# Moving the additions of the output halves: from the head of the next tick to the tail of the tick of the copies

## The chip, the cores and the metric

The kernel runs on one core of one Trainium2 chip. The metric is the device time of one execution in microseconds (us): 1191.49 us is the median of three runs of the kernel before, which lie between 1190.52 and 1192.2 us. The traces come from a profiled execution of its own. The engines are named as in the profile: PE (TensorE matrix products), PEld (its weight loads), DVE (VectorE), ACT (ScalarE), POOL (GpSimd) and SP (SyncE, which only issues DMAs).

## The reference

The kernel computes windowed attention followed by a gated feed-forward layer, all in float32. The attention has 8 batches, 8 heads, 576 positions and a head size of 64. Half of the heads see a plain window of 32 positions, the other half a dilated one (every fourth position, 128 back).

```python
scores = scale * np.matmul(q, k.transpose(0, 1, 3, 2))
scores = np.where(masks[None, :, :, :], scores, -1000000000.0)
scores = scores - np.max(scores, axis=-1, keepdims=True)
attn = np.exp(scores)
attn = attn / (np.sum(attn, axis=-1, keepdims=True) + 1e-09)
attn_out = np.matmul(attn, v)
# 4608 tokens of 512 features: heads side by side
rms = np.sqrt(np.mean(x * x, axis=-1, keepdims=True) + 1e-06)
xn = x / rms * rms_g
g = xn @ w_gate                       # 512 -> 1536
val = xn @ w_val                      # 512 -> 1536
out = (g / (1 + np.exp(-g)) * val) @ w_out   # 1536 -> 512
```

## The kernel before, in words

**Units and ticks.** The 4608 tokens are cut into 16 units of 288 tokens (half a batch each). The feed-forward layer of unit u and the attention of unit u+1 are interleaved: while TensorE multiplies with the weights of unit u, the attention of the next unit is threaded in between. The order of everything is written out by hand in the Python program. Time there is counted in ticks: a tick is one block of feed-forward products on TensorE, either `gate` (a product with a piece of w_gate, PSUM bank "g"), `val` (the same with w_val, bank "v") or `proj` (the product with a piece of w_out, four accumulators). A unit has 12 pieces and so 36 ticks.

**Order within a tick.** `later(dt, rank, fn)` puts work off to the tick dt ahead. At the start of a tick, `flush()` issues what was put off to it, in the order of the ranks; then come the tick's products on TensorE and behind them the attention's products (`attend` and `products`). As each engine works through its own instructions in the order of issue, the ranks set the order of DVE, ACT and POOL.

**Attention.** It runs in bursts, 14 per unit: one burst is a pair of heads and 72 or 96 queries. From unit 3 on a burst starts every second tick; in unit 2 every one or two ticks. For a burst whose scores are made in tick q:

- tick q: scores on TensorE (line 428), into PSUM tile `s`
- tick q+1, rank 0.7: `scores_max` on DVE (lines 307 and 312)
- tick q+2, rank 2: `scores_exp` on ACT (line 322)
- tick q+4, rank -1: `scores_norm`, a small addition and a reciprocal on DVE (lines 329 and 330) and the scaling on POOL (line 332)
- tick q+5: the transposes on TensorE (line 402), into the unused part of the bank "g" or "v"; tick q+6, rank 0.2: `untranspose`, a rounded copy on ACT (line 385) and the remainder on DVE (line 387)
- tick q+8: the product with the values on TensorE (lines 416 and 417), into PSUM tile `o`, of which there is one
- tick q+9, rank 0.5: `take` on ACT (line 357), below

**Halves.** Operands of the products are split into a part in the rounded format fp32r ("hi") and a remainder ("lo"). The product of the probabilities with the values leaves two halves side by side in `o`: that of the hi part and that of the lo part. `take` copies the second half on ACT to the SBUF tile `xraw` (two copies of 64 partitions, one per head), and DVE adds the first half to it (two additions, line 350). After that `o` is free for the next burst's product.

**Other work of DVE that the prediction speaks of.** `prod` (line 603, rank 0) multiplies gate and value, `silu` (line 590, rank 0.8) finishes the gate's activation, `q_lo` (line 290, rank 0.9) makes the remainder of the queries, and `split_weight` (line 187, rank 6) makes the remainder of a weight piece; the last stands on POOL or DVE, and only until all the weights are split, in the time of units 0 to 2. The transposes go to the bank that `silu` or `prod` reads, and are held until these have read it. The first two units compute in plain float32 and have no halves to add.

Of the kernel before, what the change touches and what calls it, by code (L numbers as in the profile page):

```python
# [14 lines left out]
ALU = mybir.AluOpType  # L15
PSUM = bass.MemoryType.PSUM

B, H, S, D = 8, 8, 576, 64
# [6 lines left out]
DIL = 4  # L25
QB = 96
NC = DM // P
NJ = FF // P
NNAT = 2
# [15 lines left out]
def geometry(u, c):  # L45


    half = u % 2
    if c < NC // 2:
        if half:  # L50
            return [(QB * i, QB * i, 0, P) for i in range(U // QB)], QB, U + W
        return [(QB * i, max(QB * i - W, 0), 0 if i else W, P if i else QB)
                for i in range(U // QB)], QB, U
    nq = U // DIL
    keys = nq + (W if half else 0)
    return [(nq * r, keys * r, 0 if half else W, keys) for r in range(DIL)], nq, keys * DIL
# [3 lines left out]
def attn_moe(ctx: ExitStack, tc: tile.TileContext, qk_in, v_in, w_gate, w_val, w_out, rms_g, outT):  # L60
# [4 lines left out]
    V, A, G, PE = nc.vector, nc.scalar, nc.gpsimd, nc.tensor  # L65
# [32 lines left out]
    def later(dt, rank, fn):  # L98
        put_off.setdefault(now[0] + dt, []).append((rank, fn))
# [123 lines left out]
    def load_v(b):  # L223

        if b is not None and b[0] >= NNAT:
            u, c, i = b
            vt = sb.tile([P, 2, D], F32, tag="vt", name=f"vt_{u}_{c}_{i}", bufs=3)
            nc.sync.dma_start(out=vt.rearrange("p a d -> p (a d)"), in_=v_in[u, c][:, i * 2 * D:(i + 1) * 2 * D])
            vs[b] = vt

    def further(b, n):

        k = everything.index(b) + n
        return everything[k] if k < len(everything) else None
# [6 lines left out]
    def split_v(b, dt):  # L241
        k = everything.index(b) % 2

        def hi():
            if k not in vparts:
                vparts[k] = [late[0].tile([P, 2, D], F32R, name=f"v{p}_{k}", bufs=1) for p in ("hi", "lo")]
            A.copy(out=vparts[k][0], in_=vs[b])  # L247

        def lo():
            vh, vl = vparts[k]  # L250
            G.tensor_tensor(out=vl, in0=vs.pop(b), in1=vh, op=ALU.subtract)  # L251
            load_v(further(b, 3))

        later(dt, 3.3, hi)
        later(dt, 5.1, lo)

    def after(u, h, n):

        k = u * H + h + n
        return divmod(k, H) if k < NU * H else None  # L260
# [37 lines left out]
    st, xraw, xsq = {}, {}, {}  # L298
# [36 lines left out]
    def take(u, c, i, o):  # L335

        blocks, nq, _ = geometry(u, c)
        if (u, c) not in xraw:
            xraw[u, c] = sb.tile([P, U], F32, tag="xraw", name=f"xraw_{u}_{c}", bufs=NC)
        x = xraw[u, c]  # L340
        if c < NC // 2:
            to = x[:, QB * i:QB * i + nq]
        else:
            to = x.rearrange("p (j r) -> p r j", r=DIL)[:, i, :]
        copy = V.tensor_copy if i % 2 and u != 1 else A.copy

        def add():
            for a in range(2):
                rows = slice(a * D, (a + 1) * D)
                V.tensor_tensor(out=to[rows], in0=o[rows, a * nq:(a + 1) * nq], in1=to[rows], op=ALU.add)  # L350

        if u < NNAT:
            for a in range(2):
                copy(out=to[a * D:(a + 1) * D], in_=o[a * D:(a + 1) * D, a * nq:(a + 1) * nq])
        else:
            for a in range(2):
                A.copy(out=to[a * D:(a + 1) * D], in_=o[a * D:(a + 1) * D, (2 + a) * nq:(3 + a) * nq])  # L357
            later(1, -0.5, lambda: add())
        if i == len(blocks) - 1:
            later(1, 2.5, lambda: square(u, c))  # L360

    def square(u, c):
        first = c == 0
        sq = sb.tile([P, U], F32, tag="xsq" if first else "tmp", name=f"sq_{u}_{c}", bufs=1 if first else 2)
        x = xraw[u, c]
        A.activation(out=sq, in_=x, func=AF.Square)
        if u == 0:
            G.tensor_scalar(out=x, in0=x, scalar1=gs[:, c:c + 1], scalar2=1.0, op0=ALU.mult, op1=ALU.mult)
        if first:
            xsq[u] = sq  # L370
        else:
            later(1, 0.4, lambda: (V if c == NC - 1 else G).tensor_tensor(out=xsq[u], in0=xsq[u], in1=sq, op=ALU.add))
# [6 lines left out]
    def untranspose(b, t_ps):  # L379
        blocks, nq, _ = geometry(*b[:2])  # L380
        n = blocks[b[2]][3]
        t_in = t_ps[:n].rearrange("k (a q) -> k a q", a=2)[:, :, :nq]
        exact = b[0] < NNAT
        st[b] = pt = sb.tile([P, 2, 2, QB], F32 if exact else F32R, tag="pt", name=f"pt_{b[0]}_{b[1]}_{b[2]}", bufs=2)
        A.copy(out=pt[:n, 0, :, :nq], in_=t_in)
        if not exact:
            V.tensor_tensor(out=pt[:n, 1, :, :nq], in0=t_in, in1=pt[:n, 0, :, :nq], op=ALU.subtract)  # L387

    def products(q, t, o, t_ps, s_tag="s", o_tag="o"):


        if q:
            s_ps = ps.tile([P, 512], F32, tag=s_tag, name=f"s_{q[0]}_{q[1]}_{q[2]}")
        if o:
            o_ps = ps.tile([P, 512], F32, tag=o_tag, name=f"o_{o[0]}_{o[1]}_{o[2]}")
            pt = st.pop(o)
        if t:
            p, _ = st.pop(t)
        def transposed(a):
            blocks, nq, _ = geometry(*t[:2])  # L400
            n = blocks[t[2]][3]
            PE.transpose(t_ps[:n, a * QB:a * QB + nq], p[:nq, a, :n], ident[:nq, :nq])  # L402

        def output(a):
            blocks, nq, _ = geometry(*o[:2])
            n = blocks[o[2]][3]
            if a:
                return
            out = o_ps[:, :2 * nq].rearrange("d (a q) -> d a q", a=2)
            if o[0] < NNAT:  # L410
                PE.matmul(out, vs.pop(o)[:n].rearrange("k a d -> k (a d)"), pt[:n, 0, :, :nq], start=True, stop=True)
                return
            vh, vl = (part[:n].rearrange("k a d -> k (a d)") for part in vparts[everything.index(o) % 2])

            both = o_ps[:, :4 * nq].rearrange("d (t a q) -> d t a q", t=2, a=2)
            PE.matmul(both, vh, pt[:n, :, :, :nq], start=True, stop=False)  # L416
            PE.matmul(out, vl, pt[:n, 0, :, :nq], start=False, stop=True)

        def scored(a):
            blocks, nq, _ = geometry(*q[:2])  # L420
            qc, kc, _, n = blocks[q[2]]
            sv = s_ps[:QB].rearrange("q (a t k) -> q a t k", a=2, t=2)
            if q[0] < NNAT:
                qr, kr = heads[q[0], 2 * q[1] + a]
                PE.matmul(sv[:nq, a, 0, :n], qr[:, qc:qc + nq], kr[:, kc:kc + n], start=True, stop=True)
                return
            qs, ks = heads[q[0], 2 * q[1] + a]
            PE.matmul(sv[:nq, a, :, :n], qs[:, qc:qc + nq], ks[:, :, kc:kc + n], start=True, stop=True)  # L428

        parts = [(b, fn, a) for b, fn in ((t, transposed), (o, output), (q, scored)) for a in range(2)]  # L430
        for b, fn, a in parts:
            if b:
                fn(a)
        if t:
            later(1, 0.2, lambda: untranspose(t, t_ps))
        if o:
            later(1, 0.5, lambda: take(*o, o_ps))
            if o[0] < NNAT:
                later(1, 9, lambda: load_v(further(o, 3)))
            far = further(o, 2)  # L440
            if far and far[0] >= NNAT:
                split_v(far, 8 if o[0] < NNAT else 1)
        if q:
            later(1, 0.7, lambda: scores_max(*q, s_ps))
            later(2, 2, lambda: scores_exp(*q))
            later(3 if q[0] < NNAT else 4, -1, lambda: scores_norm(*q))
            u, c, i = q
            nxt = after(u, 2 * c, 2)
            nb = len(geometry(u, c)[0])
            if u < NNAT:  # L450
                if u == NNAT - 1 and c == NC - 1 and i == nb - 1:
                    for a in range(2):
                        later(1, 9, lambda a=a: load(NNAT, a))
                        later(5 + a, 9, lambda a=a: split(NNAT, a, (1, 2, 2, 3), G, V))
            elif nxt and i == 0:
                split(*nxt, (1, 2, 2, 3), G, V)
                split(nxt[0], nxt[1] + 1, (2, 3, 3, 4), G, V)
# [224 lines left out]
    for n in range(ends):  # L682
# [8 lines left out]
        if n == ends - 1:  # L691
            _, v_free = gate(0, 0), val(0, 0)
# [101 lines left out]
```

## Time and profile before

| | |
|---|---|
| median of three runs | 1191.49 us (1190.52 to 1192.2) |
| the profiled execution's own time | 1190.96 us |
| its span, first to last instruction | 1189.2 us |
| busy: PE, DVE, ACT, POOL | 1131.2, 823.8, 720.1, 632.5 us |
| additions of the halves (line 350, DVE) | 392 instructions, 104.2 us busy |
| copies of the halves (line 357, ACT) | 392 instructions, 101.3 us busy |

In a row of the time order ("timeline"), the columns are the start in us, the duration in us, the engine, the line of the kernel, the operation, what it writes and reads, its shape, and how many instructions were merged in the row. Brackets at the end hold the engine's idle time before it, in us, and what it waited for. In a list of waits, the three numbers are the total in us, how often, and the longest.

### The profile page before, as it was taken

The page shows a single profiled execution, that of the slowest core. Times are in us where ns is not written, and L with a number is a line of the kernel's source. Part 1 is how long each engine was busy: PE and PEld are TensorE (multiplying, and loading weights), DVE is VectorE, ACT ScalarE, POOL GpSimd, SP SyncE. Part 2 cuts the span into 40 slices and gives each one's busy share as a digit, 9 for nine tenths or more (in the row PEclk, how much of TensorE's full clock was granted, in tenths as well). Part 3 has the DMA queues.
Part 4 walks back from the last instruction along what each step waited for, and adds up shares of the span by engine and source line. Part 5 has one row for each costly group of instructions (what it writes and reads, how often), then busy time and mean ns, then how long its engine had stood idle before and what let it go on. Part 6 is the DMA issues. An engine that isn't in the chain of part 4 may idle for free.

```text
span 1189.2 us, 25908 instructions
## 1 busy us (share of the span) xinstructions
PE 1131.2 (95%) x8296; PEld 1088.2 (92%) x8296; DVE 823.8 (69%) x2939; ACT 720.1 (61%) x2624; POOL 632.5 (53%) x1094
## 2 busy tenths in 40 slices
PE   4788888999999999999999999999999999999998
PEld 3566677999999999999999999999999999999998
DVE  4789786685858767586867767586776858687421
ACT  4667466675666657565765757566675756566321
POOL 2667466564556555464655646465554646455211
PEclk7699899999999999999999999999999999999999
DMA  5655322121312213121221212131121213120000
GB/s 151 196 181 200 93 73 58 34 85 34 92 40 79 58 38 91 37 80 39 69 60 50 88 33 75 40 89 49 48 83 34 81 37 93 40 76 17 1 21 21
DMA packets 62713, 82.19 MB, mean 69 GB/s; under 512 B 7442, under 2 KB 43282, under 8 KB 62578
## 3 DMA queue, kind: packets, MB, share of 16 engines
q1 hardware_dynamic: 61242, 79.60, 22.2%
q8 instruction: 66, 1.08, 0.4%
q10 hardware_dynamic: 1336, 0.94, 0.3%
q14 instruction: 69, 0.57, 0.2%
HBM read 71.08 MB, written 9.44 MB: 68 GB/s over the span
## 4 chain that ended last, share of the span: by engine, by line
PE 71%; DVE 18%; ACT 3%; DMA 3%; issue 2%; POOL 1%; SPq 0%; POOLq 0%; DVEq 0%; ACTq 0%
PE acc L551 7%; PE acc L552 7%; PE acc L553 7%; PE v L551 7%; PE g L551 7%; PE v L552 6%; PE v L553 6%; PE g L553 6%; PE g L552 6%; DVE qs L290 3%; PE o L416 3%; PE s L428 2%; DVE t L312 2%; DVE xraw L522 2%; PE g L402 2%
## 5 line engine op out<-in xcount | busy, mean ns | idle before, releaser
L615 POOL TENSOR_TENSOR hlo<-th,hhi 128x288 fp32r<-128x288 f32 x180 | 145.6, 809 | 230.0 <-ACT hhi L614 226.0
L332 POOL TENSOR_SCALAR t<-t,sm 96x128 f32<-96x128 f32 (+3 forms) x448 | 181.1, 416 | 85.3 <-DVE sm L330 58.6
L551 PE MATMUL v<-xhi,hi_v 128*128 128x288 f32 x720 | 220.5, 306 | 4.0 <-DVE pt L387 3.8
L551 PE MATMUL acc<-hhi,hi_o 128*128 128x288 f32 x720 | 221.0, 307 | 0.0
L551 PE MATMUL g<-xhi,hi_g 128*128 128x288 f32 x720 | 219.8, 305 | 0.3 <-DVE pt L387 0.2
L552 PE MATMUL acc<-hlo,hi_o 128*128 128x288 f32 x720 | 212.8, 296 | 0.2 <-POOL hlo L615 0.2
L552 PE MATMUL v<-xlo,hi_v 128*128 128x288 f32 x720 | 212.7, 295 | 0.0
L552 PE MATMUL g<-xlo,hi_g 128*128 128x288 f32 x720 | 212.7, 295 | 0.0
L553 PE MATMUL g<-xhi,lo_g 128*128 128x288 f32 x720 | 212.6, 295 | 0.0
L553 PE MATMUL acc<-hhi,lo_o 128*128 128x288 f32 x720 | 212.5, 295 | 0.0
L553 PE MATMUL v<-xhi,lo_v 128*128 128x288 f32 x720 | 212.3, 295 | 0.0
L614 ACT CAST hhi<-th 128x288 fp32r<-128x288 f32 x180 | 77.9, 433 | 169.6 <-DVE th L603 163.3
L322 ACT ACTIVATE t<-t,sm 96x128 f32<-96x128 f32 (+3 forms) x448 | 166.7, 375 | 16.4 <-DMA v<-in_v_dram 12.9
L251 POOL TENSOR_TENSOR vlo<-vt,vhi 128x128 fp32r<-128x128 f32 x196 | 94.1, 480 | 128.2 <-ACT vhi L247 104.1
L585 ACT ACTIVATE th<-g 128x288 f32<-128x288 f32 x180 | 73.9, 411 | 121.9 <-PE g L553 92.3
L551 PEld LDWEIGHTS v<-xhi,hi_v 128*128 128x128 f32 x720 | 135.2, 188 | 7.2 <-DVE pt L387 7.2
L350 DVE TENSOR_TENSOR xraw<-o,xraw 64x96 f32<-64x96 f32 (+1 forms) x392 | 104.2, 266 | 47.9 <-ACT xraw L357 45.0
L552 PEld LDWEIGHTS acc<-hlo,hi_o 128*128 128x128 f32 x720 | 135.8, 189 | 0.5 <-POOL hlo L615 0.5
L551 PEld LDWEIGHTS g<-xhi,hi_g 128*128 128x128 f32 x720 | 135.2, 188 | 0.6 <-DVE pt L387 0.3
L552 PEld LDWEIGHTS v<-xlo,hi_v 128*128 128x128 f32 x720 | 135.7, 188 | 0.0
L552 PEld LDWEIGHTS g<-xlo,hi_g 128*128 128x128 f32 x720 | 135.6, 188 | 0.0
L553 PEld LDWEIGHTS acc<-hhi,lo_o 128*128 128x128 f32 x720 | 135.4, 188 | 0.0
(120 smaller groups left out, 2668.1 us busy)
## 6 DMA issues: line engine op xcount, KB each, us to landing
qk<-in_qk_dram SPq DMA_DIRECT2D x56, 288.0 KB, 2.8
vt<-in_v_dram SPq DMA_DIRECT2D x196, 64.0 KB, 1.9
qk<-in_qk_dram SPq DMA_DIRECT2D x28, 352.0 KB
out_dram<-ot SPq DMA_DIRECT2D x64, 144.0 KB, 2.0
qk<-in_qk_dram SPq DMA_DIRECT2D x28, 304.0 KB, 2.8
raw_g<-in_w_gate_dram SPq DMA_DIRECT2D x12, 512.0 KB, 3.1
raw_v<-in_w_val_dram SPq DMA_DIRECT2D x12, 512.0 KB, 4.2
raw_o<-in_w_out_dram SPq DMA_DIRECT2D x12, 512.0 KB
```

The source lines that it names most:

```text
L251: G.tensor_tensor(out=vl, in0=vs.pop(b), in1=vh, op=ALU.subtract)
L290: eq.tensor_tensor(out=qs[D:], in0=qr[D:], in1=qs[D:], op=ALU.subtract)
L322: A.activation(out=t[:nq, a, :n], in_=t[:nq, a, :n], func=AF.Exp, scale=-1.0, bias=sm[:nq, a:a + 1], accum_out=sm[:nq, 2 + a:3 + a])
L332: G.tensor_scalar(out=t[:nq, a, :n], in0=t[:nq, a, :n], scalar1=sm[:nq, 2 + a:3 + a], scalar2=1.0, op0=ALU.mult, op1=ALU.mult)
L350: V.tensor_tensor(out=to[rows], in0=o[rows, a * nq:(a + 1) * nq], in1=to[rows], op=ALU.add)
L416: PE.matmul(both, vh, pt[:n, :, :, :nq], start=True, stop=False)
L551: PE.matmul(out, wh[:, cc, :], xh, start=start, stop=False)
L552: PE.matmul(out, wh[:, cc, :], xl, start=False, stop=False)
L553: PE.matmul(out, wl[:, cc, :], xh, start=False, stop=stop)
L585: A.activation(out=t, in_=g, func=AF.Tanh, scale=0.5)
L614: A.copy(out=hi, in_=t)
L615: G.tensor_tensor(out=lo, in0=t, in1=hi, op=ALU.subtract)
```

## The change

The two additions of a burst are no longer put off from `take` to the next tick at rank -0.5. They are put off, together with `take`, to the same tick as the copies, at rank 4. At the old place they stood behind `scores_norm` (rank -1) and ahead of everything else of tick q+10. At the new one they stand in tick q+9 behind `silu` and `q_lo`, ahead of the weight split (rank 6) of that tick, and ahead of `scores_norm` of tick q+10. What is added, and by which instructions, stays as it is, and for units 0 and 1 nothing differs.

```diff
@@ take
-
-        def add():
-            for a in range(2):
-                rows = slice(a * D, (a + 1) * D)
-                V.tensor_tensor(out=to[rows], in0=o[rows, a * nq:(a + 1) * nq], in1=to[rows], op=ALU.add)
-
         if u < NNAT:
             for a in range(2):
                 copy(out=to[a * D:(a + 1) * D], in_=o[a * D:(a + 1) * D, a * nq:(a + 1) * nq])
         else:
             for a in range(2):
                 A.copy(out=to[a * D:(a + 1) * D], in_=o[a * D:(a + 1) * D, (2 + a) * nq:(3 + a) * nq])
-            later(1, -0.5, lambda: add())
         if i == len(blocks) - 1:
             later(1, 2.5, lambda: square(u, c))
+
+    def add(u, c, i, o):
+        _, nq, _ = geometry(u, c)
+        x = xraw[u, c]
+        to = x[:, QB * i:QB * i + nq] if c < NC // 2 else x.rearrange("p (j r) -> p r j", r=DIL)[:, i, :]
+        for a in range(2):
+            rows = slice(a * D, (a + 1) * D)
+            V.tensor_tensor(out=to[rows], in0=o[rows, a * nq:(a + 1) * nq], in1=to[rows], op=ALU.add)
@@ products
         if o:
             later(1, 0.5, lambda: take(*o, o_ps))
+            if o[0] >= NNAT:
+                later(1, 4, lambda: add(*o, o_ps))
```

## The prediction

> **What bounds the kernel now.** I read the page first, then the busy times by stretch, then the waits of PE, then the time order around every wait of PE. The page says which engine is nearest to full:
>
> ```profile
> span 1189.2 us, 25908 instructions
> PE 1131.2 (95%) x8296; PEld 1088.2 (92%) x8296; DVE 823.8 (69%) x2939; ACT 720.1 (61%) x2624; POOL 632.5 (53%) x1094
> ```
>
> PE is busy 95% of the span, so a shorter time can come only out of PE's idle time. The busy times by stretch (window, its length, then busy time and instruction count of PE, PEld, DVE, ACT, POOL, the granted clock, the DMA share and GB/s) show where that is:
>
> ```profile
> 160.00:230.00 70.00, 61.29 (x454) 58.06 (x453) 47.69 (x168) 47.26 (x168) 43.13 (x71) 1.00 0.19 54
> 230.00:1110.00 880.00, 872.09 (x6721) 860.19 (x6721) 633.09 (x2352) 564.16 (x2119) 484.23 (x885) 1.00 0.20 59
> ```
>
> The additions are these (durations in ns: shortest, median, longest; first and last start):
>
> ```profile
> L350 DVE TENSOR_TENSOR xraw<-o,xraw x392: 226/261/298, 163.4 to 1110.6; 64x72 f32<-64x72 f32 x112, 64x96 f32<-64x96 f32 x84
> ```
>
> In the first stretch, where unit 2's attention runs together with the last weight splits, PE idles 70.00 - 61.29 = 8.71 us; in the 880 us behind it, 7.91 us. So 16.6 us is all that any change of this kind could win. The waits say how much of it hangs on the additions (rows of PE, then of DVE):
>
> ```profile
> PE o L416 <- DVE xraw L350: 4.5, 6, 1.4
> ...
> DVE xraw L350 <- ACT xraw L357: 45.0, 45, 1.8
> ```
>
> Six times the next burst's product with the values waits until the additions have read the one `o` tile: 4.5 us. The last row is the other side: at its old place the addition holds DVE 45 times, 45.0 us, for the copies of ACT. These are the single waits of PE that I go through below:
>
> ```profile
> 175.70 0.27 PE L402 MATMUL v<-ident,t 96*128 96x96 f32 x1 [0.64 <-DVE th L603]
> ...
> 183.68 0.41 PE L416 MATMUL o<-pt,vhi 128*128 128x384 f32 x1 [0.53 <-DVE xraw L350]
> ...
> 201.14 0.37 PE L416 MATMUL o<-pt,vhi 72*128 72x288 f32 x1 [0.30 <-DVE xraw L350]
> ...
> 205.41 0.37 PE L416 MATMUL o<-pt,vhi 72*128 72x288 f32 x1 [0.42 <-DVE xraw L350]
> ...
> 206.01 0.40 PE L551 MATMUL g<-xhi,hi_g 128*128 128x288 f32 x1 [0.17 <-DVE pt L387]
> ...
> 216.61 0.37 PE L416 MATMUL o<-pt,vhi 72*128 72x288 f32 x1 [1.40 <-DVE xraw L350]
> ...
> 526.72 0.41 PE L416 MATMUL o<-pt,vhi 128*128 128x384 f32 x1 [0.97 <-DVE xraw L350]
> ...
> 801.45 0.41 PE L416 MATMUL o<-pt,vhi 128*128 128x384 f32 x1 [0.83 <-DVE xraw L350]
> ```
>
> **The change, part by part.** No instruction is added or removed; 392 additions stay, and they issue no DMA and pass no work of SP, POOL or ACT. On DVE's queue they pass at most two things: a weight remainder (rank 6 of the tick of the copies) and the normalisation (rank -1 of the next tick). Where neither stands between the old and the new place, the order of DVE is word for word the same.
>
> *Past the weight remainders.* DVE's order around three of them:
>
> ```profile
> 172.34 0.43 DVE L590 SCALAR_TENSOR_TENSOR th<-th,g 128x288 f32<-128x288 f32 x1
> 173.53 1.10 DVE L187 TENSOR_TENSOR lo_g<-f_g,hi_g 128x512 fp32r<-128x512 f32 x1 [0.76 <-ACT hi_g L186]
> 174.55 0.51 DVE L350 TENSOR_TENSOR xraw<-o,xraw 64x96 f32<-64x96 f32 x2
> 175.10 0.46 DVE L603 TENSOR_TENSOR th<-th,v 128x288 f32<-128x288 f32 x1
> ...
> 201.64 0.45 DVE L590 SCALAR_TENSOR_TENSOR th<-th,g 128x288 f32<-128x288 f32 x1 [0.64 <-ACT th L585]
> 203.82 0.69 DVE L187 TENSOR_TENSOR lo_o<-f_o,hi_o 128x512 fp32r<-128x512 f32 x1 [1.73 <-POOL vlo L251]
> ...
> 204.71 0.56 DVE L350 TENSOR_TENSOR xraw<-o,xraw 64x72 f32<-64x72 f32 x2
> 205.29 0.46 DVE L603 TENSOR_TENSOR th<-th,v 128x288 f32<-128x288 f32 x1
> ...
> 213.91 0.46 DVE L590 SCALAR_TENSOR_TENSOR th<-th,g 128x288 f32<-128x288 f32 x1 [1.11 <-ACT th L585]
> 215.29 0.69 DVE L187 TENSOR_TENSOR lo_o<-f_o,hi_o 128x512 fp32r<-128x512 f32 x1 [0.92 <-POOL vlo L251]
> 215.90 0.57 DVE L350 TENSOR_TENSOR xraw<-o,xraw 64x72 f32<-64x72 f32 x2
> ```
>
> In each, DVE ends `silu` and then idles 0.76, 1.73 and 0.92 us ahead of the remainder, with the additions queued behind it. The copies they need are long done:
>
> ```profile
> 170.78 0.47 ACT L357 COPY xraw<-o 64x96 f32<-64x96 f32 x2
> ...
> 201.62 0.58 ACT L357 COPY xraw<-o 64x72 f32<-64x72 f32 x2
> ...
> 213.78 0.57 ACT L357 COPY xraw<-o 64x72 f32<-64x72 f32 x2
> ```
>
> At the new place the additions fill that idle time. First case: they run at 172.8; the remainder starts as before, when its own operand is there, and `prod` comes 175.10 - 174.55 = 0.55 us earlier; PE's wait at 175.70 shrinks from 0.64 to 0.09. Second: they run from 202.2 (copies) to 202.8, PE could start at 205.41 - 0.42 = 204.99, so 0.42 goes; `prod` and the `untranspose` behind it come 0.58 earlier, which clears the 0.17 at 206.01. Third: they end at 214.37 + 0.57 = 214.94, PE is free at 216.61 - 1.40 = 215.21, so all 1.40 goes. Together 0.55 + 0.42 + 0.17 + 1.40 = 2.54 us. The waits at 183.68 and 201.14 I leave: there neither a remainder nor a normalisation stands directly ahead of the addition. Where a remainder and an addition both stay ahead of a late `prod`, the transposes that wait for it gain nothing either.
>
> *Past the normalisation.* From unit 3 on a burst starts every second tick, so the old place, tick q+10, is also tick q+4 of the third burst after it: the normalisation of that burst stood ahead in 11 of a unit's 14 bursts (the last three have no third burst after them). Two of PE's waits are of this kind:
>
> ```profile
> 525.64 0.31 DVE L329 TENSOR_SCALAR sm<-sm 72x2 f32<-72x2 f32 x1
> ...
> 526.07 0.50 DVE L350 TENSOR_TENSOR xraw<-o,xraw 64x96 f32<-64x96 f32 x2
> ...
> 799.25 0.46 DVE L290 TENSOR_TENSOR qs<-qk,qs 64x288 fp32r<-64x288 f32 x1 [1.07 <-ACT qs L285]
> 799.73 0.95 DVE L329 TENSOR_SCALAR sm<-sm 72x2 f32<-72x2 f32 x1
> ...
> 800.80 0.50 DVE L350 TENSOR_TENSOR xraw<-o,xraw 64x96 f32<-64x96 f32 x2
> ```
>
> ```profile
> 799.12 0.47 ACT L357 COPY xraw<-o 64x96 f32<-64x96 f32 x2
> ```
>
> The copies for the second end at 799.59, before L329 starts, and those for the first do so too. The additions move up by 526.07 - 525.64 = 0.43 us and by 800.80 - 799.73 = 1.07 us. The first wait falls from 0.97 to 0.54, the second (0.83) goes: 0.43 + 0.83 = 1.26 us. What the swap costs is a normalisation that ends some 0.5 us later. Behind it wait POOL's scaling and then the transposes; the tightest kind in the steady stretch:
>
> ```profile
> 513.43 0.71 POOL L332 TENSOR_SCALAR t<-t,sm 96x128 f32<-96x128 f32 x2 [0.39 <-DVE sm L330]
> ...
> 516.00 0.33 PE L402 MATMUL v<-ident,t 96*128 96x96 f32 x2
> ```
>
> From the end of the scaling, 514.14, to the transposes there are 1.86 us of slack, so 0.5 us is covered; it would show only if the cover shrank by 1.4 us. `prod`, `untranspose` and `silu` come behind both in either order. POOL's later work moves by up to 0.5 us; I price that at nothing, bounded below.
>
> DVE's stalls decide whether the swap costs DVE itself. The additions took between 226 and 298 ns in all 392 cases, while the tiny L329 took 0.31 and 0.95 us above. So the additions can use a time in which L329 would stall.
>
> By the Trainium skill, "SBUF — State Buffer", section "Who interferes with whom", a VectorE instruction with at most one SBUF input outside the two-port modes does not contend with GpSimd, while a two-port tensor_scalar does, and the later of the two then blocks for a whole instruction. The trace agrees for the additions, one of whose inputs lies in PSUM. By the rule the sum stands; were an addition stalled like L329 at 799.73, the 0.83 us would be lost again and the sum be 2.97.
>
> **Sum:** 2.54 + 1.26 = 3.80 us. Against the profiled execution's own 1190.96 us (span 1189.2 and 1.8 around it) that gives 1187.16. The median shown is 0.53 us above that execution, so against it I forecast 1191.49 - 3.80 = **1187.7 us**. If the two waits that I left and the remaining 0.54 went too, the gain would be 3.80 + 0.53 + 0.30 + 0.54 = 5.17 us.
>
> **The rivals.**
>
> *Half is given back.* PE, earlier in unit 2, could meet a DVE that is not earlier, and the 2.54 us would return as new waits by 230 us. Left would be 1.26: 1190.2 us. For it: the remainders wait for ACT and POOL, which need not be earlier. Against it: soon behind 216.61 DVE itself waits for PE,
>
> ```profile
> 220.58 0.42 DVE L307 TENSOR_TENSOR t<-s,mask 96x256 f32<-96x256 f32 x1 [0.97 <-PE s L428]
> ```
>
> so it follows when PE is earlier.
>
> *POOL runs into `q_lo`.* POOL's reads come up to 0.5 us later and may now hold the queries' remainder:
>
> ```profile
> L290 DVE TENSOR_TENSOR qs<-qk,qs 64x288 fp32r<-64x288 f32 x112 | 86.6, 773 | 6.1 <-ACT qs L285 2.7
> ```
>
> Its mean is 773 ns, against 0.46 us at 799.25: 0.31 us of stall each already. Another 0.31 us at one tight place in each of 13 units would be 4.0 us, and the time 1191.7. Against it: POOL waits at its scaling (idle 0.39 us above) and starts nothing meanwhile.
>
> *Slower: the addition blocks the queue.* At the tail it waits for ACT with the normalisation and `prod` behind it. Where DVE ran the normalisation ahead of such a wait, that time is no longer hidden: for example here,
>
> ```profile
> 276.63 0.59 DVE L350 TENSOR_TENSOR xraw<-o,xraw 64x72 f32<-64x72 f32 x2 [0.27 <-ACT xraw L357]
> ```
>
> a 0.27 us wait grows by the normalisation. Taken with the 0.43 us from 525.64 to 526.07 at all 45 waits, that is 19.4 us of DVE. It decides once more than 3.8 of these, a fifth, reach PE; with half, 9.7 - 3.8 = 5.9 us is lost: 1197.4. Against it: by the time order of DVE only the last such burst of a unit (13 units) and three in unit 2 have both a normalisation and a wait behind it, 16 x 0.43 = 6.9 us, with slack as above before it reaches PE.
>
> The Trainium skill's "PSUM — Partial Sum Buffer", section "Engine vs sequencer instructions", calls VectorE's queue a strict FIFO; the 45.0 us row, an engine held by one instruction, agrees. By it alone, with no slack counted, all 19.4 us would come on top: 1207.1.
>
> *It does nothing.* If the copies ended no earlier than the old place was reached, the additions would end when they do now: 1191.5. Against it: the rows of ACT above.
>
> **How the numbers follow.** Forecast 0.55, half given back 0.20, POOL 0.10, slower 0.10, nothing 0.05. A measurement of this kernel can tell about 0.2%, 2.4 us. The forecast counts as faster, bar a small part, as does a bit of the second case: faster 0.60, within 0.30, slower 0.10. The range runs from a little under 1191.49 - 5.17 = 1186.3 to the POOL case, 1185.3 to 1191.8; it leaves out the slower case and tails.
>
> **What would show it.** In the profile after, `PE o L416 <- DVE xraw L350` should fall from 4.5 us to about 1.4 and lose 216.61's row; PE's idle time at 160 to 230 should fall from 8.7 to about 6.2; the additions should stand ahead of L187 and L329. DVE's wait for the copies may grow, without harm. I am wrong if PE waits anew for L402 or L551 in the steady stretch, or if L290's mean rises well above 773 ns.

## The result and the profile after

The changed kernel takes 1182.01 us in the median (1181.43 to 1182.95), against 1191.35 us for the kernel before beside it: a ratio of 0.9922, interval 0.9905 to 0.994. The gain is 9.3 us where 3.8 were forecast. The profiled execution took 1182.95 us. The page of the profile after begins:

```profile
span 1181.2 us, 25911 instructions
...
PE 1128.6 (96%) x8296; PEld 1089.9 (92%) x8296; DVE 814.4 (69%) x2939; ACT 719.4 (61%) x2624; POOL 638.7 (54%) x1094
```

The span is 8.0 us shorter, but PE is busy only 2.6 us less, and the idle time that the page leaves it fell from 1189.2 - 1131.2 = 58.0 to 52.6 us, by 5.4. The busy times by stretch of the kernel after, in the columns of the prediction's fence:

```profile
160.00:230.00 70.00, 63.83 (x465) 61.07 (x465) 49.62 (x175) 48.57 (x173) 44.78 (x72) 0.98 0.20 59
230.00:1110.00 880.00, 874.62 (x6772) 865.87 (x6771) 625.16 (x2354) 565.13 (x2121) 490.34 (x888) 1.00 0.20 59
```

In the long stretch PE's idle time went from 7.91 to 5.38 us, 2.5 us less. But the number of PE's instructions in the same 880 us rose from 6721 to 6772. At 880 / 6772 = 0.130 us each the 51 more are worth 6.6 us. In the short stretch 11 more are worth 1.4 us. Together that is the 8.0 us of the span. So the count of instructions in a stretch of fixed length sees the gain, and in the long stretch PE's idle time sees less than half of it.

The idle time of the *weight loads* sees it as well: 880 - 860.19 = 19.81 us before, 880 - 865.87 = 14.13 after, 5.7 us less. The Trainium skill, "Perfetto Trace Analysis", section "Identifying the Most-Contended Engine", says that the busy time of matmuls doesn't measure how near a kernel is to its limit, because they are pipelined, and that the busy share of the weight loads does. The trace agrees: PE's idle time fell by 2.5 us, that of the weight loads by 5.7, where the count of instructions gives 6.6.

The groups of instructions of the same long stretch name the place. The columns after the bar are busy time, mean ns, idle time just ahead of these instructions, and what ended it. Before, one row of PE and three of its weight loads:

```profile
L416 PE MATMUL o<-pt,vhi 128*128 128x384 f32 (+3 forms) x182 | 59.0, 324 | 2.3 <-DVE xraw L350 1.8
...
L551 PEld LDWEIGHTS v<-xhi,hi_v 128*128 128x128 f32 x616 | 115.7, 188 | 5.4 <-DVE pt L387 5.4
...
L416 PEld LDWEIGHTS o<-pt,vhi 128*128 128x128 f32 (+3 forms) x182 | 34.2, 188 | 6.3 <-ACT t L322 3.7 <-issue 1.2 <-ACT pt L385 0.3
L402 PEld LDWEIGHTS g<-ident,t 96*128 96x128 f32 (+2 forms) x234 | 27.6, 131 | 7.7 <-POOL xlo L532 3.3 <-issue 2.0 <-POOL vlo L251 0.4
```

After:

```profile
L554 PEld LDWEIGHTS v<-xhi,hi_v 128*128 128x128 f32 x622 | 116.8, 188 | 5.3 <-DVE pt L388 5.3
...
L417 PEld LDWEIGHTS o<-pt,vhi 128*128 128x128 f32 (+3 forms) x182 | 34.3, 188 | 0.0
L403 PEld LDWEIGHTS g<-ident,t 96*128 96x128 f32 (+2 forms) x234 | 27.5, 131 | 8.4 <-POOL xlo L535 3.3 <-issue 2.2 <-POOL vlo L251 0.4
```

Ahead of the weight load of the value product (line 416, now 417) 6.3 us of idle time went to nothing. The matmul row of the same product showed 2.3 us. The releasers named in the weight loads' row (`t L322`, "issue") are not the additions; as the experiments below show, the size is to be trusted here and the name is not.

How a wait can be there and not be printed is seen in one burst of the steady stretch. In the time order of the kernel before:

```profile
470.85 0.73 DVE L329 TENSOR_SCALAR sm<-sm 72x2 f32<-72x2 f32 x1
...
471.69 0.56 DVE L350 TENSOR_TENSOR xraw<-o,xraw 64x72 f32<-64x72 f32 x2
...
472.10 0.30 PE L553 MATMUL g<-xhi,lo_g 128*128 128x288 f32 x1
...
472.40 0.37 PE L416 MATMUL o<-pt,vhi 72*128 72x288 f32 x1
472.61 0.23 PE L417 MATMUL o<-pt,vlo 72*128 72x144 f32 x1
```

The same burst after:

```profile
467.83 0.59 DVE L361 TENSOR_TENSOR xraw<-o,xraw 64x72 f32<-64x72 f32 x2
468.44 0.17 DVE L329 TENSOR_SCALAR sm<-sm 72x2 f32<-72x2 f32 x1
...
469.08 0.30 PE L556 MATMUL g<-xhi,lo_g 128*128 128x288 f32 x1
469.21 0.30 PE L417 MATMUL o<-pt,vhi 72*128 72x288 f32 x1
469.34 0.23 PE L418 MATMUL o<-pt,vlo 72*128 72x144 f32 x1
```

After, the product starts 0.13 us behind its forerunner, although that one is printed with 0.30 us: the printed duration overlaps the next start. Before, the additions end at 472.25, the product starts 0.30 us behind its forerunner, and the one behind it 0.21 us instead of 0.13 later. That is 0.17 + 0.08 = 0.25 us lost, and since 472.10 + 0.30 = 472.40 no idle time is printed. The distances of starts of every value product from unit 3 to unit 15 can be added up in the same way, against the undisturbed distance (0.13 us to the product, and 0.13 or 0.17 us, by its shape, from it to the next): before, 7.2 us were lost at 27 places, and after, none. Two of these places, those of the printed waits, lost 1.2 and 1.1 us; the other 25 lost 0.09 to 0.34 us each. So the printed waits were the longest of a wait that came about twice in each of the 13 units.

### The profile page after: what moved, and what is told of

It reads as the page before. It is cut to its first block, busy times and chain, and to the rows that moved or that the text cites. A ratio compares the mean times of both kernels' runs of the same rounds, so it can differ in the third digit from the quotient of the medians.

```text
span 1181.2 us, 25911 instructions
## 1 busy us (share of the span) xinstructions
PE 1128.6 (96%) x8296; PEld 1089.9 (92%) x8296; DVE 814.4 (69%) x2939; ACT 719.4 (61%) x2624; POOL 638.7 (54%) x1094
## 4 chain that ended last, share of the span: by engine, by line
PE 77%; DVE 15%; ACT 2%; DMA 2%; issue 2%; POOL 1%; SPq 0%; POOLq 0%; DVEq 0%; ACTq 0%
PE acc L554 8%; PE v L554 7%; PE acc L555 7%; PE acc L556 7%; PE g L554 7%; PE v L555 7%; PE v L556 7%; PE g L555 7%; PE g L556 7%; DVE qs L290 3%; PE s L429 3%; PE o L417 2%; PE g L403 2%; DVE xraw L525 2%; DVE t L312 2%
## 5 line engine op out<-in xcount | busy, mean ns | idle before, releaser
L332 POOL TENSOR_SCALAR t<-t,sm 96x128 f32<-96x128 f32 (+3 forms) x448 | 184.4, 423 | 129.7 <-DVE sm L330 104.7
L322 ACT ACTIVATE t<-t,sm 96x128 f32<-96x128 f32 (+3 forms) x448 | 166.8, 375 | 18.6 <-DMA k<-in_qk_dram 13.8
L361 DVE TENSOR_TENSOR xraw<-o,xraw 64x96 f32<-64x96 f32 (+1 forms) x392 | 106.7, 272 | 61.6 <-ACT xraw L351 56.6
L588 ACT ACTIVATE th<-g 128x288 f32<-128x288 f32 x180 | 73.9, 410 | 120.6 <-PE g L556 88.2
L556 PEld LDWEIGHTS g<-xhi,lo_g 128*128 128x128 f32 x720 | 135.9, 189 | 0.0
```

The costliest lines, as they stand in the source:

```text
L322: A.activation(out=t[:nq, a, :n], in_=t[:nq, a, :n], func=AF.Exp, scale=-1.0, bias=sm[:nq, a:a + 1], accum_out=sm[:nq, 2 + a:3 + a])
L332: G.tensor_scalar(out=t[:nq, a, :n], in0=t[:nq, a, :n], scalar1=sm[:nq, 2 + a:3 + a], scalar2=1.0, op0=ALU.mult, op1=ALU.mult)
L556: PE.matmul(out, wl[:, cc, :], xh, start=False, stop=stop)
L588: A.activation(out=t, in_=g, func=AF.Tanh, scale=0.5)
```

## The experiments

Diffs here are against the changed kernel, whose line numbers hold unless said otherwise. Each ratio is to the kernel before, timed on the same chip. The theory under test: nearly all of the unforecast gain is the value product's wait for the additions, most of it unprinted, and it goes where the additions stand ahead of the normalisation. The rivals: the gain comes from unit 2; or from DVE's time, as the normalisation is stalled less at its new place.

**Only unit 2 at the new place.** The later units go back to the old one.

```diff
-                later(1, 4, lambda: add(*o, o_ps))
+                later(*((1, 4) if o[0] == NNAT else (2, -0.5)), lambda: add(*o, o_ps))
```

> Only the additions of unit 2 stand at the new place (behind the copies, ahead of the weight remainder and of the normalisation); from unit 3 on they stand at the old one. First theory (the gain is the idle time of PE that the profile prints): 2.54 us of the gain are here, so about 1188.8 us. Second theory (a late addition also costs PE time that is not printed as idle, and most of it lies in the later units): about 1.5 to 2.8 us, 1188.6 to 1189.9 us. This run alone does not part them; it gives the first term of the sum.

Measured: 1187.77 us, ratio 0.9976 (0.9965 to 0.9987), that is 1190.63 - 1187.77 = 2.9 us. The forecast's unit 2 term was 2.54 us.

**Only the later units at the new place.**

```diff
-                later(1, 4, lambda: add(*o, o_ps))
+                later(*((1, 4) if o[0] > NNAT else (2, -0.5)), lambda: add(*o, o_ps))
```

> Only the additions from unit 3 on stand at the new place; unit 2 keeps the old one. First theory (printed idle time only): 1.26 us gained, about 1190.1 us. Second theory (PE also loses up to about 0.16 us unprinted at each late addition and some 0.08 us behind it): the start-to-start intervals of the product with the values give 7.2 us, so about 1184.2 us.

Measured: 1185.4 us, ratio 0.9957 (0.9943 to 0.9971), 5.2 us. The forecast's term for these units was 1.26 us. The two halves add up to 8.1 us of the whole's 9.3, within their intervals.

**Ahead of the normalisation, but in the next tick.** All additions pass the normalisation and no weight remainder.

```diff
-                later(1, 4, lambda: add(*o, o_ps))
+                later(2, -1.5, lambda: add(*o, o_ps))
```

> The additions of all units pass the normalisation only: they stay in the tick after the copies, at rank -1.5, behind the weight remainder. First theory: 1.26 us gained, about 1190.1 us. Second theory: all of the later units' gain, as no weight remainder is left there, and little in unit 2: about 1184 to 1185 us.

Measured: 1184.79 us, ratio 0.995 (0.9934 to 0.9967), 5.8 us. Busy times by stretch, of the kernel with only unit 2 moved, then of this one:

```profile
230.00:1110.00 880.00, 873.57 (x6731) 861.85 (x6730) 632.18 (x2345) 562.83 (x2113) 482.35 (x882) 1.00 0.19 59
```

```profile
230.00:1110.00 880.00, 874.32 (x6771) 865.69 (x6770) 626.20 (x2357) 564.67 (x2123) 491.29 (x889) 1.00 0.20 59
```

In the long stretch unit 2's move brings 10 of the 51 instructions more, and passing the normalisation alone brings 50. (They needn't add exactly, since a shorter start shifts the stretch.) The distance from the first value product of unit 3 to that of unit 15, which holds the same work in every kernel, says it without that shift: 823.1 us before, 822.3 with only unit 2 moved, 817.1 with only the later units moved, 817.2 here and 817.0 in the changed kernel. So what the later units gain is the swap with the normalisation and nothing else of the new place.

**Directly behind the copies.** The additions are put so far forward that they stand ahead of the masking and maxima of the scores, `silu` and `q_lo` in the copies' tick (ranks 0.7, 0.8 and 0.9). This is the forecast's slower rival, made as strong as it can be.

```diff
-                later(1, 4, lambda: add(*o, o_ps))
+                later(1, 0.55, lambda: add(*o, o_ps))
```

> The additions stand directly behind the copies of their tick, at rank 0.55, ahead of the row maxima, silu and the queries' remainder. If an addition that waits for ACT at the head of DVE's queue does harm (the slower rival of the prediction), the maxima and silu come late and PE waits for silu ahead of the transposes: 3 us or more above the changed kernel, 1185 us or more. If there is slack for that everywhere, it equals the changed kernel, about 1182 us. DVE's wait for the copies should grow far beyond 57 us in either case.

Measured: 1236.08 us, ratio 1.0381 (1.0363 to 1.0399), 45 us slower. Its list of waits, of PE and of DVE:

```profile
PE g L403 <- DVE sm L329: 32.9, 46, 1.0
...
DVE xraw L361 <- ACT xraw L351: 221.2, 179, 2.6
```

and its weight loads of the transposes over the whole span:

```profile
L403 PEld LDWEIGHTS g<-ident,t 96*128 96x128 f32 (+2 forms) x280 | 30.2, 131 | 65.4 <-POOL vlo L251 31.2 <-issue 24.3 <-POOL xlo L535 3.3
```

DVE now stands 179 times, 221 us, in front of the copies, with `silu`, `q_lo` and the normalisation queued behind, and the transposes lose 65.4 us where the changed kernel loses 20.8. The row of PE names the normalisation (line 329), but it is `silu` that the transposes wait for: all 46 of them start 0.15 us behind the end of a `silu`, while POOL's last scaling ended 1.3 us or more before (at 317.55 us, for example, `silu` ended at 317.40 and the scaling at 315.52). Line 329 is only the next instruction of DVE's queue. The rival's mechanism is real. It decides when the addition stands ahead of `silu`, not when it stands behind it: the changed kernel has 52 waits for the copies, 56.6 us in all, and gains all the same.

**Is it the addition's end, or DVE's time?** The changed kernel also has 9.4 us less of DVE busy time, so DVE's load could be the cause. A copy out of `o` (one head's first half) to a spare tile that nobody reads is put ahead of the additions of units 3 to 15, once at the old place and once at the new one.

```diff
+    spare = cst.tile([D, QB], F32, name="spare")
@@ add
+        if u > NNAT:
+            V.tensor_copy(out=spare[:D, :nq], in_=o[:D, :nq])
```

At the old place (with `later(2, -0.5, ...)`):

> Additions at the old place, as in the kernel before; from unit 3 on one more DVE instruction per burst stands ahead of them, a copy of 64x96 out of the same tile o (about 0.25 us) into a spare tile that nothing reads. If the release of o is what costs (second theory), each burst whose product with the values starts less than 0.25 us after the release pays: from the starts in the trace before, lateness grows from 5.2 to about 13 us, so about 8 us above the kernel before, 1199 us. If DVE's total time were what counts, it is 13 x 14 x 0.25 = 45 us of DVE work, and the same amount more at either place.

Measured: 1192.71 us, ratio 1.0022 (1.0011 to 1.0032), 2.2 us slower than before; the profiled execution, the longest of eight, is 5.8 us longer than the profiled one of before. At the new place:

> The same extra copy, with the additions at the new place. Second theory (release of o): every release in the trace after lies at least 0.34 us ahead of the need, so 0.25 us is covered and the time is the changed kernel's, about 1182 us (at most 1183). If DVE's total time counted, the loss against the changed kernel would be as large as that of the old place, about 8 us.

Measured: 1185.64 us, ratio 0.9965 (0.9951 to 0.9978); that is some 3.6 us above the changed kernel. Groups of weight loads over the whole span, old place first (the lines stand three further down: 420 is the value product, 406 the transposes):

```profile
L420 PEld LDWEIGHTS o<-pt,vhi 128*128 128x128 f32 (+3 forms) x196 | 36.8, 188 | 14.0 <-ACT t L323 6.6 <-issue 5.8 <-ACT xraw L352 0.7
L406 PEld LDWEIGHTS g<-ident,t 96*128 96x128 f32 (+2 forms) x280 | 32.7, 131 | 20.0 <-issue 9.7 <-POOL xlo L538 3.3 <-POOL lo_g L188 1.6
```

```profile
L420 PEld LDWEIGHTS o<-pt,vhi 128*128 128x128 f32 (+3 forms) x196 | 37.0, 189 | 1.2 <-ACT xraw L352 0.7 <-ACT t L323 0.2
L406 PEld LDWEIGHTS g<-ident,t 96*128 96x128 f32 (+2 forms) x280 | 32.3, 131 | 22.8 <-issue 9.9 <-POOL lo_g L188 3.6 <-POOL xlo L538 3.3
```

For comparison, before and after:

```profile
L416 PEld LDWEIGHTS o<-pt,vhi 128*128 128x128 f32 (+3 forms) x196 | 36.8, 188 | 9.8 <-ACT t L322 3.7 <-issue 3.5 <-ACT xraw L357 0.7
L402 PEld LDWEIGHTS g<-ident,t 96*128 96x128 f32 (+2 forms) x280 | 32.8, 131 | 18.1 <-issue 7.4 <-POOL xlo L532 3.3 <-POOL lo_g L187 1.6
```

```profile
L417 PEld LDWEIGHTS o<-pt,vhi 128*128 128x128 f32 (+3 forms) x196 | 37.1, 189 | 0.9 <-ACT xraw L351 0.7
L403 PEld LDWEIGHTS g<-ident,t 96*128 96x128 f32 (+2 forms) x280 | 32.6, 131 | 20.8 <-issue 9.5 <-POOL xlo L535 3.3 <-POOL lo_g L187 1.6
```

At the old place a longer addition makes the value product wait more, 9.8 to 14.0 us; at the new place the product does not notice, 0.9 to 1.2 us. That is what a gain by the addition's earlier end requires, and DVE's load alone would not tell the places apart. But both sizes were wrong. The old place paid far less than expected, 2.2 us in the median, where the trace has 4.8 us more from unit 3's first value product to unit 15's (827.9 us). In part that is because the copy overlaps the addition behind it and puts it off by 0.16 us, not 0.25 (at 519.80 us the copy starts, at 519.96 the addition); the rest is open, and the eight runs (1191.92 to 1196.74 us) spread more than the effect is large. The new place was not free: the transposes lost 2.0 us more there, and the medians 3.6 us. It is `silu` that carries this to the transposes: from unit 3 on, all transposes that start late, 34 in the changed kernel and 34 here, start 0.15 us behind the end of a `silu`, and by the distances of starts they lose 6.0 us there and 7.3 here. So more DVE time costs about the same at either place, by different ways, and this experiment alone does not put DVE's load aside. It bounds it: 25.7 us more of DVE's busy time cost 3.6 us at the new place, and at that rate the 9.4 us less would be worth 1.3 us, which is an estimate. The 7.2 us that the value product lost cover the later units' gain without it.

**Unit 2's other queue-holder.** The weight remainder on DVE is put off to the next tick, behind `prod` and `untranspose`.

```diff
-        e.tensor_tensor(out=lo, in0=f, in1=hi, op=ALU.subtract)
+        def rest():
+            e.tensor_tensor(out=lo, in0=f, in1=hi, op=ALU.subtract)
+
+        if e is V:
+            later(1, 0.3, rest)
+        else:
+            rest()
```

> The changed kernel with DVE's weight remainders put off to rank 0.3 of the next tick, behind prod and untranspose. They then hold up neither. Second theory: the waits of PE that are left in unit 2 behind them (0.75, 0.21 and 1.81 us printed at 167, 175 and 198 us, and about 0.2 us more each) shrink: 2 to 3 us, about 1179.5 us. If the remainders only get in the way of the row maxima instead, the time stays at 1182 us.

Measured: 1180.03 us, ratio 0.9917 (0.9904 to 0.993). The interval overlaps the changed kernel's, so this shows neither a gain nor its absence.

**What is late next.** The 5.3 us that are left ahead of line 554 wait for `untranspose` (line 388), which stands behind the normalisation. For one burst of each unit from 3 on the normalisation is put behind `untranspose` (rank 0.2).

```diff
-            later(3 if q[0] < NNAT else 4, -1, lambda: scores_norm(*q))
+            late_norm = q[0] > NNAT and q[1:] == (0, 1)
+            later(3 if q[0] < NNAT else 4, 0.25 if late_norm else -1, lambda: scores_norm(*q))
```

> The changed kernel with the normalisation of the second burst of each unit from unit 3 on at rank 0.25 (it was -1), behind the untranspose remainder that PE waits for once a unit (0.15 to 0.25 us printed). First theory (printed idle only): 13 x 0.2 = 2.6 us, about 1179.4 us. Second theory (about 0.16 us unprinted and some 0.1 us behind each wait come on top): 13 x 0.45 = 5.9 us, about 1176 us. If the later normalisation holds up the transposes instead, no gain or a loss.

Measured: 1178.51 us, ratio 0.9903 (0.9889 to 0.9916), between the times expected. Groups of weight loads of the long stretch (lines from 550 on stand one further down):

```profile
L555 PEld LDWEIGHTS v<-xhi,hi_v 128*128 128x128 f32 x623 | 117.0, 188 | 0.0
...
L403 PEld LDWEIGHTS g<-ident,t 96*128 96x128 f32 (+2 forms) x234 | 27.5, 131 | 10.9 <-POOL xlo L536 7.9 <-POOL vlo L251 0.4 <-issue 0.2
```

The 5.3 us went wholly, and 10.9 - 8.4 = 2.5 us came back as a wait of the transposes: 2.8 us less in all, beside some 3.5 us less in the medians. What came back is not the price of the later normalisation. In 13 waits of the transposes, one in each unit, PE starts 0.15 us behind the end of `silu`, and POOL's last scaling ended 1.1 us or more before. PE comes earlier and meets the next thing that is late, `silu`.

**`silu` earlier.** On top of that, `silu` goes ahead of the masking and maxima of the scores (rank 0.7) from unit 1 on, so that the bank of the gate comes free for the transposes earlier.

```diff
-        later(1, 0.8, silu)
+        later(1, 0.65 if u else 0.8, silu)
```

> The kernel with the late normalisation of the second burst, and silu at rank 0.65 instead of 0.8 in every tick of units 1 to 15, ahead of the row maxima. The transposes wait for silu (5.2 us printed in that kernel, 13 times once a unit). If silu's place in the queue is what makes it late, 4 to 6 us less than that kernel's 1178.5 us, about 1173.5 us. If silu waits for ACT's tanh ahead of the maxima in many ticks (the queue blocked, as with the additions directly behind the copies), the time rises above 1182 us.

Measured: 1169.83 us, ratio 0.9829 (0.9816 to 0.9843). This version beats both kernels, 1189.77 - 1169.83 = 19.9 us below the one before. Busy times by stretch and groups of weight loads of the long stretch:

```profile
230.00:1110.00 880.00, 879.76 (x6857) 877.65 (x6855) 626.41 (x2360) 568.56 (x2127) 491.88 (x890) 1.00 0.19 59
```

```profile
L555 PEld LDWEIGHTS v<-xhi,hi_v 128*128 128x128 f32 x628 | 117.9, 188 | 0.4
...
L417 PEld LDWEIGHTS o<-pt,vhi 128*128 128x128 f32 (+3 forms) x182 | 34.2, 188 | 1.1 <-ACT t L322 0.8 <-issue 0.2
L403 PEld LDWEIGHTS g<-ident,t 96*128 96x128 f32 (+2 forms) x233 | 30.1, 131 | 0.5
```

PE issues 136 instructions more than before in the same 880 us, 136 x 880 / 6857 = 17.5 us, and the weight loads idle 2.35 us where they idled 19.81. The 19.9 us are more than could be had at all by the forecast's reading, which allowed 16.6. The 10.9 us ahead of the transposes fell to 0.5: it was `silu` that they waited for.

**`silu` earlier in one tick of each unit only**, from unit 3 on and with the later normalisation; and the same with the weight remainder put off as above.

```diff
+            tight.add(now[0] + 4)
...
-        later(1, 0.8, silu)
+        later(1, 0.55 if now[0] + 1 in tight else 0.8, silu)
```

> The same, but silu is moved (to rank 0.55) only in the one tick of a unit in which PE waits for it. By the start-to-start intervals of the transposes, some 0.4 to 0.65 us in each of 13 units: 5 to 6 us less than 1178.5 us, about 1173 us; by printed idle only 13 times 0.35 = 4.5 us, about 1174 us. If another wait takes its place at once, 1178.5 us.

> The last kernel and, in addition, the weight remainders of DVE put off behind prod and untranspose. If the remainders' place matters, 1 to 2 us less than the kernel without; if the stretch of the weight splits is bound otherwise, equal to it.

Measured: 1172.37 us, ratio 0.985 (0.9836 to 0.9863), and 1172.33 us, 0.9852 (0.9839 to 0.9865). The one tick brings most of `silu`'s gain: 1178.51 to 1172.37 us, of the 8.7 us to 1169.83. The remainder's place brings nothing measurable on top.

**The changed kernel again**, beside these:

> The changed kernel once more, on the same chip as these. Both theories: 0.992 of the kernel before, about 1182 us. The stretch from unit 3's first product with the values to the last unit's should take 817 us as in the first trace, against 823 in the kernel before.

Measured: 1181.96 us, ratio 0.9925 (0.9912 to 0.9939). The stretch took 817.0 us, against 823.1 in the trace of the kernel before.

## Why the prediction was wrong

**The step that failed is "So 16.6 us is all that any change of this kind could win", with the idle time of PE (8.71 and 7.91 us) as the measure.** It took the printed idle time for all the time in which PE could have issued more. A late start of up to 0.30 - 0.13 = 0.17 us prints nothing, and the product behind it is late too. In the long stretch 2.3 us were printed ahead of the value products, 6.3 us stood ahead of their weight loads, and 7.2 us were lost by the distances of starts. With the late normalisation and `silu` early in every tick, 17.5 us were won in a stretch for which the forecast allowed 7.91.

**The term "0.43 + 0.83 = 1.26 us" for the normalisation was mis-sized for this reason.** Its mechanism was right: the additions passed the normalisation, and the value product stopped waiting. The move of the later units alone measured 5.2 us, and the swap with the normalisation alone brought 50 of the 51 instructions. The forecast counted the two places with a printed wait; there were 27, and the 25 others lost 4.9 us together. Replacing 1.26 by 5.2 gives 2.54 + 5.2 = 7.7 us and 1190.96 - 7.7 + 0.53 = 1183.8, still 1.8 above what was measured, which the intervals of the parts (0.9943 to 0.9971 is 3.4 to 6.8 us) allow.

**Of the first wait, 0.54 us were to remain, and it went wholly.** The forecast moved the addition up by the normalisation's length only. In the time order of before, then after, for that burst:

```profile
524.18 1.43 DVE L290 TENSOR_TENSOR qs<-qk,qs 64x288 fp32r<-64x288 f32 x1 [0.89 <-ACT qs L285]
```

```profile
520.16 0.46 DVE L290 TENSOR_TENSOR qs<-qk,qs 64x288 fp32r<-64x288 f32 x1 [0.17 <-ACT qs L285]
...
520.65 0.52 DVE L361 TENSOR_TENSOR xraw<-o,xraw 64x96 f32<-64x96 f32 x2
521.21 0.39 DVE L329 TENSOR_SCALAR sm<-sm 72x2 f32<-72x2 f32 x1
...
522.29 0.34 PE L417 MATMUL o<-pt,vhi 128*128 128x384 f32 x1
```

Before, `q_lo` took 1.43 us just ahead of the old place. After, it took 0.46 in the same burst, and the addition ended 1.12 us before PE came.

**The term "2.54 us" for the weight remainders had the right size.** The move of unit 2 alone measured 2.9 us (interval 0.9965 to 0.9987, 1.5 to 4.2 us). From unit 2's first value product to unit 3's the traces have 76.7 us with only the later units moved and 73.9 in the changed kernel, 2.8 us less (75.5 in the kernel before, in whose trace the clock did not fall in this stretch; see the last section). Its parts came out unevenly. In the time order of after, around the third of them:

```profile
204.26 0.69 DVE L187 TENSOR_TENSOR lo_o<-f_o,hi_o 128x512 fp32r<-128x512 f32 x1 [1.01 <-POOL vlo L251]
...
214.34 0.59 DVE L361 TENSOR_TENSOR xraw<-o,xraw 64x72 f32<-64x72 f32 x2
215.07 0.37 PE L417 MATMUL o<-pt,vhi 72*128 72x288 f32 x1
215.25 0.69 DVE L187 TENSOR_TENSOR lo_o<-f_o,hi_o 128x512 fp32r<-128x512 f32 x1 [0.33 <-POOL vlo L251]
```

The additions stand ahead of the remainder, in time in which DVE would have idled, and the 1.40 us ahead of 216.61 are gone, as said. So is the 0.42 at 205.41. Of the 0.64 at 175.70, 0.21 us is left instead of 0.09. The 0.17 at 206.01 was not cleared (0.15 is left): there the remainder starts at 204.26 instead of 203.82, since what it waits for on POOL comes later, and `prod` behind it gained nothing. Why POOL is later there was not tried. The wait at 183.68, which the forecast left alone, stayed at 0.53.

**The normalisation's later end cost nothing, as said, and DVE's own time fell.** Groups of DVE, before and after:

```profile
L329 DVE TENSOR_SCALAR sm<-sm 72x2 f32<-72x2 f32 (+1 forms) x224 | 84.0, 375 | 7.1 <-ACT t L322 5.4
```

```profile
L290 DVE TENSOR_TENSOR qs<-qk,qs 64x288 fp32r<-64x288 f32 x112 | 80.7, 720 | 4.4 <-ACT qs L285 0.4
...
L329 DVE TENSOR_SCALAR sm<-sm 72x2 f32<-72x2 f32 (+1 forms) x224 | 64.0, 286 | 12.6 <-ACT t L322 7.5
```

The normalisation's mean fell from 375 to 286 ns, which the forecast left out of its sum; what that is worth by itself was not measured. The additions took between 241 and 298 ns at the new place, so they were not stalled there as line 329 had been. The weight loads of the transposes, which come behind the normalisation and POOL's scaling, idle 8.4 us in the long stretch where they idled 7.7. But from unit 3 on all transposes that start late, 30 before and 34 after, start 0.15 us behind the end of a `silu`, and POOL's last scaling ended 1.1 us or more before. So the 0.7 us more are a wait for `silu`, and the swap's price was rightly put at nothing.

**The rivals.** *Half is given back* is wrong: PE's waits in unit 2 did not return. *POOL runs into `q_lo`* is wrong: `q_lo`'s mean went from 773 to 720 ns. *The addition blocks the queue* was rightly put low for this place: DVE's wait for the copies grew from 45.0 to 56.6 us and the kernel is faster. The experiment with rank 0.55 shows the harm, 45 us, for another place. *It does nothing* is wrong by the result. Of the signs named in advance, `PE o L416 <- DVE xraw L350` was to fall from 4.5 to about 1.4 us; in the list of waits after it is

```profile
PE o L417 <- DVE xraw L361: 0.5, 1, 0.5
...
DVE xraw L361 <- ACT xraw L351: 56.6, 52, 1.8
```

PE's idle time at 160 to 230 us was to fall to about 6.2 and fell to 70 - 63.83 = 6.17. Of the 4.5 us it was the 0.53 at 183.68 alone that stayed. No new printed wait of line 403 or 554 arose in the steady stretch: from 230 to 1110 us PE has 8 and 12 of them before (lines 402 and 551), 7 and 12 after.

## What to carry to other kernels

Where matmuls are pipelined, a wait of the tensor engine is sized by the distance of starts, by the number of instructions in a stretch of fixed length, or by the idle time ahead of the weight loads, not by the idle time that is printed ahead of the matmul: one short wait in every round of a steady loop can be nearly invisible there. The order of an engine's queue is then best set by which of its instructions frees a PSUM bank that the tensor engine comes to next: here the addition ahead of the normalisation, and `silu` ahead of the work on the scores. An instruction that waits for another engine should not be put ahead of the one that frees the next bank, even where its own result is wanted early; here that cost 45 us.

## What the runs showed of the hardware that was not expected

Behind a pause of PE in unit 2 the clock fell in some executions. Busy times by stretch, before and then after:

```profile
196.00:198.00 2.00, 0.40 (x4) 0.16 (x2) 1.92 (x5) 0.00 (x0) 0.57 (x1) 1.00 0.33 67
...
200.00:202.00 2.00, 1.70 (x14) 1.49 (x13) 1.31 (x8) 1.95 (x9) 1.66 (x4) 1.00 0.00 0
```

```profile
196.00:198.00 2.00, 0.19 (x3) 0.16 (x3) 1.89 (x6) 0.24 (x1) 0.23 (x1) 1.00 0.44 107
...
200.00:202.00 2.00, 2.00 (x10) 2.00 (x10) 0.62 (x4) 1.05 (x5) 1.65 (x3) 0.50 0.04 12
```

Both kernels have PE nearly idle from 196 to 198 us; the pause is 1.8 us long in both (196.40 to 198.24 us, and 196.07 to 197.88). After, the granted clock was 0.50 from 200 to 202 us and PE issued 10 instructions that fill the time, where 2.00 / 0.13 would be 15. That is about 0.13 x 5 = 0.7 us in these 2 us, an estimate, which the profiled execution of before does not pay. The change does not bring it about: the run with only the later units moved, whose unit 2 is that of the kernel before, has 0.17 us of PE's work from 196 to 198 us and the clock at 0.50 from 200 to 202; the run with the longer additions at the old place has a pause of 2.0 us (196.88 to 198.93) and the clock at 1.00 behind it. So the length of the pause alone does not decide. The Trainium skill, "TensorE: Matmul & The Clock Gate", section "Part 1: The HAM clock gate", describes a clock that is halved after an idle window which runs freely, so that it is open which pause meets it. The trace agrees in the 0.50; the window itself no run here shows.
